# Block sums of batch 0 in other pairs, and a new order of issue, in a fused sparse attention and two-layer product on one core

## The chip, the core and the metric

The kernel runs on one core of a Trainium2 chip. The core has TensorE (PE) for matrix products, with weight loads shown apart as PEld; VectorE (DVE) and ScalarE (ACT) for elementwise work; GpSimd (POOL) and SyncE (SP), which here mostly issue transfers. The metric is the device time of one execution in microseconds (us); less is better. One execution in a set is also profiled, and from it come the page, the timeline and the waits quoted below. Its span runs from the first to the last recorded instruction.

## The reference

Four batches, 8 heads, 768 positions of 64 numbers. Each query attends to the keys less than 16 positions away and to 24 block keys (the elementwise maximum of 32 keys each, with weight log 32); a block's value is the mean of its 32 values. The result, 3072 rows of 512, goes through two products with a hard-swish between them.

```python
k_sum = k.reshape(B, H, nb, block, D).max(axis=3)       # block = 32, nb = 24
v_sum = v.reshape(B, H, nb, block, D).mean(axis=3)
scores_l = scale * q @ k^T, kept where |i - j| < 16
scores_s = scale * q @ k_sum^T + log(block)
a = softmax(concat(scores_l, scores_s))
x = a @ concat(v, v_sum)                                # 3072 x 512 after the heads are put side by side
h = x @ w_in                                            # 512 x 2048
out = (h * clip(h + 3, 0, 6) / 6) @ w_out               # 2048 x 512
```

## The kernel before

The work is built as a list of small steps, each with a name, an engine, and what it reads and writes. The string ORDER (lines 29 to 72) lists all steps by name; `Plan.run` walks it with written-out costs, gives each step its buffer and a planned begin, and sorts the steps by that begin. Each engine then runs its steps in the resulting order, in which it may wait but never overtakes. `:A` or `:D` behind a name puts a step that either engine can do on ACT or DVE. The names, with b a batch:

- K and Q, V, h, B with a batch number: loads of k, q, v, of the 32 rows of v ahead of each window (halo), and of v by blocks (batch 3 only), all issued by POOL. I and O are the weights of the two products (lines 499 and 505). Lines 447, 456, 467, 490, 493 and 725 are where loads of k and q, of v, of halos and of blocks are issued. Eight loads are in flight at most.
- k and q (b = 0): transposes on PE of raw keys and queries, with the copies out of PSUM and the maximum over blocks (line 559). For batches 1 and 2 DVE transposes instead (lines 617 and 623), and w makes the block maxima (778) and their copies; for batch 3 a crossbar transfer on SP's queue does it (599 and 608).
- s: scores on PE (649 for batch 0, 683 for the others), the exponential on ACT (660, 689), the band mask on DVE (691).
- u: block sums of v on PE (702 and 748) with their copies and spreads over the windows; U: the sums of batch 3 on DVE (735).
- v: attention times values (813 to 817 and 844), the normalisation on DVE (851, 852), and the transpose of x: on PE for batch 0 and the second half of batch 1, by a crossbar transfer on SP (line 857) for the rest. y (line 861) is a two-element copy on POOL that waits for the first crossbar transfer; the loads behind it start after that transfer has landed.
- F with stage and column group: the first product (928) into a PSUM buffer S, ACT's relu (934), DVE's product (936). A stage is half a batch, so stages 4 and 5 are batch 2. Two F steps of four matmuls each fill one S, called a pair below.
- G with stage and row group: the second product (950) in steps of four matmuls, the copy of the finished rows into one of four buffers ot (517, by ACT or DVE), and the store on SP (961, 962).

PSUM holds three S buffers of two banks and two single ones, h. PE has filler matmuls (line 1049) in the planned gaps of the first 27 us.

At the start, batch 0 is loaded and its attention computed while the weights arrive. From then on PE alternates between F and G of the finished stages and the scores, sums and values of the next batch. The loads of batches 1 to 3 run in one long queue behind. The crossbar transfer of x of stage 4 (v20.6 in ORDER) is the first of batch 2; F40 is its first reader. SP's queue holds the crossbar transfers and the stores in one order.

For batch 0 the block sums of four head pairs are made in two bursts of 24 matmuls (`vsum_first`, from line 983), each for two pairs:

```python
for cs in ((0, 2), (1, 3)):
    vsum_first(cs)
```

Of the kernel before, what the change touches and what calls it, by code (L numbers as in the profile page):

```python
# [9 lines left out]
F32 = mybir.dt.float32  # L10
# [5 lines left out]
D = 64  # L16
# [14 lines left out]
c.9 e.3 k01.1 k03.0 k02.0 q030.0 q020.0 k03.3:D c.4 q030.1:D k01.3:A k01.2:A q000.0 q010.0 k02.3:A k03.2:A k02.2:A V03.0  # L31
k03.1 k02.1 k02.4:D k01.4:D k00.0 q020.1:A q000.1:A k00.3:A s010.0 s030.0 q010.1:A s010.1 s010.2 s020.0 c.3 V01.0 V00.0 V02.0
I0.0 I2.0 I3.0 K10.0 I1.0 K13.0 K11.0 K12.0 O0.0 n.0:D k03.4:D s020.1 s030.1 s020.2 s030.2 k00.2:D k00.1 k00.4:D s000.0
q031.0 q001.0 q031.1:D q001.1:D h030.0:D h031.0:D h011.0:D h010.0:D s001.0 s000.1 s000.2 s001.1 q011.0 s001.2 s011.0 q021.0
q021.1:A q011.1:A s021.0 s031.0 s031.1 s021.1 s011.1 s031.2 s011.2 u01.0 h000.0:D u03.0:D u03.1:D u00.0 u01.1:A s021.2
u00.1:A u01.2:D h020.0:D u00.2:D u02.0:A u01.3:A u02.1:A h001.0:A u00.3:D h021.0:D O1.0 Q10.0 O2.0 Q11.0 Q13.0 Q12.0 v00.0
v01.0 v00.1 v02.0 v01.1 v02.1 v00.2 v00.3 v01.2 v02.2 v01.3 v00.4 v02.3 v03.3 v03.0 e.4 v03.1 v00.5:A v01.4 v02.4 v01.5:D
v02.5:A F00.0 F00.1 F00.2 F00.3 F00.4 F00.5 F00.6 v03.2 v03.4 v03.5 v03.6 F02.0 F02.1 F00.7 v03.7:A F02.2 F00.8 F00.9 v03.8
F00.10 F00.11 F00.12 F00.13 F02.4 F02.5 F00.14 c.5 F02.3 F00.15 F03.0 v03.9:A F02.6 F03.1 F03.2 F02.7 F03.3 F01.4 v03.10
v03.11:D F01.5 F01.6 F01.7 F03.4 F03.5 F03.6 F03.7 F10.0 F10.1 F10.2 F10.4 F10.5 F10.6 F10.3 F10.7 F01.0 F01.1 F11.4 F11.5  # L40
F01.2 k10.0 k13.0 F11.6 F01.3 F11.7 F11.0 k12.0 k11.0 G02.0 G10.0 F11.1 F11.2 F11.3 F13.0 F12.4 F12.5 F13.1 F13.2 F13.3 G02.1
w1.0 F12.6 F12.7 F12.0 F12.1 G10.1 F12.2 F12.3 G02.2 F13.4 F13.5 G01.0 F13.6 G10.2 O3.0 G11.0 G11.1 G11.2 G01.1 G01.2 G01.3
# [12 lines left out]
s230.2 u2.4:D u2.6:D s210.1 s200.1 s240.1 s240.2 u2.8:A s210.2 G22.0 F22.4 F22.5 s220.2 v20.0 v20.3 v20.1 v20.4 v20.2 v20.5
# [3 lines left out]
G21.5 k3e1.0 G30.5 k3e0.0 F40.5 F50.0 G20.3 F50.1 F50.4 F50.5 U3.4:A F40.6 F50.2 G20.4:A u3.4:D F40.7 F50.6 F52.4 F52.5  # L59
G22.4:D w3.3:D F50.3 F50.7 F52.6 F52.7 F42.4 F42.5 F53.4 F53.5 G40.0 F51.0 F51.1 u3.7:A F42.6 F53.6 w3.4:A u3.6:A w3.0 F53.7  # L60
F42.7 q3x1.0 G22.5 G32.5 q3x0.0 F51.2 F51.3 u3.1:A F51.4 F51.5 F51.6 u3.5:A F52.0 F52.1 F52.2 G41.0 G41.1 G40.1 G41.2 w3.1
F51.7 F52.3 w3.2:A s300.0 s300.1 s320.0 s350.0 s350.1 s320.1 G40.2 G41.3 G40.3 s350.2 G41.4:D G40.4:D s300.2 s310.0 u3.2:A
s310.1 s310.2 s320.2 u3.3:D s330.0 s340.0 s330.1 s340.1 G52.0 G52.1 G52.2 v33.3 v33.0 v33.1 v33.2 v33.4 F53.0 F53.1 u3.0:A
# [170 lines left out]
def kernel(  # L234
# [461 lines left out]
    def vsum_first(cs):  # L696
        T = Buf(("h", "S"))

        def mms():
            for t in range(NQ):  # L700
                for i, c in enumerate(cs):
                    nc.tensor.matmul(bank(T)[BLK * i:BLK * i + BLK, 0:2 * D], ind[:, t], vaug[0][0:WIN, 2 * c:2 * c + 2, t, 0:D],
                                     start=(t == 0), stop=(t == NQ - 1))
        plan.at(f"u0{cs[0]}")
        op("PE", mm(NQ, 2 * D), mms, form="sums", r=["ind"] + [(n, 0, c) for n in ("v", "vz") for c in cs], w=[T], alloc=T,
           touch=[rows0[c, x] for c in cs for x in range(2)])
        for i, c in enumerate(cs):
            spread_first(c, i, T)
# [385 lines left out]
```

## Time and profile before

| | us |
|---|---|
| three runs | 218.68, 216.0, 215.9 |
| median | 216.0 |
| the profiled execution, whole | 217.25 |
| its span | 215.6 |
| granted clock of PE | 0.999 of full speed |
| matmuls on PE | 2082 |

In the page a group of instructions is given by line, engine, operation and what it reads and writes; behind the count stand the busy time, the mean duration in ns, and the idle time before them with the engine that ended it. "issue" means that the profile shows nothing that the engine waited for. The timeline gives the start, the duration, the engine and line, and merges neighbours of one kind.

The stages can be read from the busy time in stretches (busy us and instructions of PE, PEld, DVE, ACT, POOL; then the granted clock, the share of the transfer engines, and GB/s):

```profile
0.00:10.00 10.00, 8.46 (x82) 3.76 (x82) 5.88 (x22) 5.49 (x12) 8.62 (x19) 1.00 0.90 123
20.00:30.00 10.00, 9.48 (x208) 7.37 (x203) 9.18 (x22) 6.81 (x12) 3.48 (x5) 1.00 1.71 186
50.00:60.00 10.00, 10.00 (x49) 4.57 (x47) 9.93 (x13) 3.54 (x6) 4.75 (x5) 1.00 2.35 151
100.00:110.00 10.00, 8.45 (x173) 4.78 (x172) 5.86 (x12) 8.64 (x10) 2.59 (x4) 1.00 1.76 139
120.00:130.00 10.00, 7.87 (x47) 4.60 (x48) 6.30 (x7) 4.54 (x6) 0.00 (x0) 1.00 0.79 164
150.00:160.00 10.00, 10.00 (x138) 5.28 (x136) 7.18 (x12) 7.43 (x9) 0.00 (x0) 1.00 0.15 55
```

PE is busy throughout most stretches; it has gaps at the start, between 100 and 110, and between 120 and 130.

### The profile page before, as it was taken

What the parts mean: (1) busy time and instruction counts of PE and PEld (TensorE: products, weight loads), DVE (VectorE), ACT (ScalarE), POOL (GpSimd) and SP (SyncE); (2) the same over time, 40 slices, a digit from 0 to 9 for tenths busy, and PEclk for the clock granted to TensorE, in tenths of its full rate; (3) what the DMA queues carried; (4) which work ended last, traced back from release to release, by engine and by line L of the source; (5) the groups of instructions that cost most, each with busy time, mean ns of one, the idle gap of its engine ahead of it and who ended that gap; (6) DMA issues with size and microseconds to landing.
All of it is one profiled execution on the core that took longest, in us unless ns stands there. A gap on an engine that the chain in (4) does not pass through costs nothing.

```text
span 215.6 us, 4886 instructions
## 1 busy us (share of the span) xinstructions
PE 204.8 (95%) x2082; PEld 115.7 (54%) x2082; DVE 154.0 (71%) x236; ACT 115.7 (54%) x163; POOL 69.2 (32%) x84
## 2 busy tenths in 40 slices
PE   7989999999999999999799599999999999999993
PEld 2555776555446665555455265655555555665442
DVE  6697887879988899997568579985785453633321
ACT  5679665533399567367980154798921541551101
POOL 7999335455446209779142000000000000000000
PEclk9999999999999999999999999999999999999999
DMA  4999999999999979999939999720223600100234
GB/s 68 184 156 195 182 159 159 181 138 157 147 122 149 112 131 135 177 163 162 171 28 148 123 197 152 124 49 2 100 42 83 170 0 3 49 0 15 97 126 155
DMA packets 120598, 25.40 MB, mean 118 GB/s; under 512 B 111424, under 2 KB 117440, under 8 KB 120576
## 3 DMA queue, kind: packets, MB, share of 16 engines
q0 software_dynamic: 102656, 15.26, 106.9%
q1 hardware_dynamic: 17920, 9.83, 19.4%
q8 instruction: 16, 0.26, 0.5%
q14 instruction: 6, 0.05, 0.1%
HBM read 30.51 MB, written 6.29 MB: 171 GB/s over the span
## 4 chain that ended last, share of the span: by engine, by line
PE 87%; DMA 4%; DVE 4%; issue 2%; ACT 1%; SPq 1%; DVEq 0%; ACTq 0%
PE S L928 38%; PE h L950 27%; PE S L950 8%; DMA out_dram<-ot 4%; PE h L1049 3%; PE S L844 3%; PE S L683 2%; DVE vaug L521 1%; PE h L538 1%; PE S L638 1%; PE S L649 1%; DVE qwide L852 1%; SPq L857 1%; ACT at L660 0%; PE h L910 0%
## 5 line engine op out<-in xcount | busy, mean ns | idle before, releaser
L928 PE MATMUL S<-x,win 128*128 128x384 bf16 (+1 forms) x544 | 88.2, 317 | 3.0 <-ACT ot L517 1.4
L934 ACT ACTIVATE r<-S 128x768 f32<-128x768 f32 x64 | 51.3, 810 | 56.6 <-PE S L928 53.8
L936 DVE SCALAR_TENSOR_TENSOR g<-r,S 128x768 bf16<-128x768 f32 x64 | 59.6, 947 | 21.0 <-ACT r L934 20.8
L928 PEld LDWEIGHTS <-win 128*128 128x128 bf16 x544 | 50.9, 98 | 37.1 <-issue 2.1
L950 PE MATMUL h<-wout,g 128*128 128x512 bf16 (+2 forms) x304 | 68.3, 365 | 0.0
L950 PEld LDWEIGHTS <-g 128*128 128x128 bf16 x416 | 38.5, 98 | 39.5
L950 PE MATMUL S<-wout,g 128*128 128x512 bf16 (+1 forms) x112 | 23.9, 356 | 0.0
L689 ACT ACTIVATE at<-S 120x1024 bf16<-120x1024 f32 x18 | 17.3, 1024 | 1.8 <-PE S L683 1.7
L467 POOL DMA_DIRECT2D vaug<-in_v_dram x16 | 15.4, 965 | 5.6 <-issue 4.1
L691 DVE TENSOR_TENSOR at<-at,mask 96x1024 bf16<-96x1024 bf16 x18 | 11.8, 680 | 4.4 <-ACT at L689 4.3
L456 POOL DMA_DIRECT2D nat<-in_q_dram x8 | 10.5, 1317 | 13.7 <-issue 9.0
L517 ACT COPY ot<-h 128x512 f32<-128x512 f32 (+2 forms) x12 | 6.5, 542 | 15.0 <-PE h L950 15.0
L456 POOL DMA_DIRECT2D nat<-in_k_dram x8 | 10.6, 1339 | 4.1 <-issue 4.1
L517 ACT COPY vaug<-vs 24x768 bf16<-24x768 bf16 x14 | 11.6, 828 | 0.3
L778 DVE TENSOR_REDUCE red<-kb 128x48 bf16<-128x1536 bf16 x6 | 10.5, 1745 | 0.0
L517 DVE COPY ot<-h 128x512 f32<-128x512 f32 x7 | 4.7, 686 | 7.6 <-PE h L950 4.7
L1049 PE MATMUL h<-g 128*128 128x512 bf16 x25 | 8.6, 486 | 1.5 <-DVE g L327 1.5
L517 ACT COPY ot<-S 128x512 f32<-128x512 f32 x3 | 1.8, 585 | 13.3 <-DMA out_dram<-ot 9.8
L517 DVE COPY ot<-S 128x512 f32<-128x512 f32 (+1 forms) x4 | 2.4, 592 | 7.8 <-PE S L950 7.8
L521 DVE TENSOR_TENSOR vaug<-vaug 32x768 bf16<-32x768 bf16 (+2 forms) x22 | 7.8, 413 | 0.1
L735 DVE TENSOR_REDUCE total<-nat 128x32 f32<-128x1024 bf16 x4 | 7.6, 1900 | 0.0
L852 DVE TENSOR_TENSOR xm<-S,rc 128x768 bf16<-128x768 f32 x8 | 7.5, 945 | 0.1
(111 smaller groups left out, 172.5 us busy)
## 6 DMA issues: line engine op xcount, KB each, us to landing
out_dram<-ot SPq DMA_DIRECT2D x19, 256.0 KB, 2.3
vaug<-in_v_dram POOLq DMA_DIRECT2D x16, 192.0 KB, 7.4
win<-in_moe_w_in_dram POOLq DMA_DIRECT2D x4, 512.0 KB, 10.8
wout<-in_moe_w_out_dram POOLq DMA_DIRECT2D x4, 512.0 KB, 17.0
nat<-in_k_dram POOLq DMA_DIRECT2D x10, 192.0 KB, 9.0
nat<-in_q_dram POOLq DMA_DIRECT2D x10, 192.0 KB, 13.2
out_dram<-ot SPq DMA_DIRECT2D x4, 224.0 KB, 2.6
nat<-in_k_dram POOLq DMA_DIRECT2D x6, 128.0 KB, 6.9
```

The lines of the kernel that those rows point to most:

```text
L456: op("POOL", 1.35, over=0.01, fn=lambda src=src, name=name, hs=hs, ds=ds, rows=rows: nc.gpsimd.dma_start(out=raw[b % 2][name][rows], in_=s ...
L467: op("POOL", 0.945, lambda: nc.gpsimd.dma_start(out=o[BLK:WIN, lo:hi, 0:D], in_=rows[:, lo:hi]), w=[("v", b % 2, c)], dma=1.28, els=1536)
L517: {"ACT": nc.scalar.copy, "DVE": nc.vector.tensor_copy, "POOL": nc.gpsimd.tensor_copy}[eng](o, i)
L521: nc.vector.tensor_tensor(o, i, i, op=ALU.max)
L689: op("ACT", 1.02, lambda: nc.scalar.activation(odds[0:KEYS, :, w], X.slot[0:KEYS], AF.Exp, scale=scl), r=[X], w=[("atg", k)])
L691: op("DVE", 0.69, lambda: nc.vector.tensor_tensor(odds[0:WIN, :, w].rearrange("p j (t c) -> p j t c", c=QB), odds[0:WIN, :, w].rearrange(" ...
L778: nc.vector.tensor_reduce(red.slot[:].rearrange("x (p u e n) -> x e u p n", p=NP, u=NS, e=2)[:, e], w[:, n * e:n * e + n, BLK:WIN].rearran ...
L928: nc.tensor.matmul(h.slot[:, f, lo * 128:hi * 128].rearrange("p (u c) -> p u c", c=128), w_in_sb[:, kt, (ft + f) * 128:(ft + f + 1) * 128] ...
L934: op("ACT", 0.81, lambda: nc.scalar.activation(r.slot[:], h.slot[:, :, 0:HALF], AF.Relu, bias=0.5, scale=1.0 / 6.0), r=[h], w=[r], alloc=r)
L936: op("DVE", 0.955, lambda: nc.vector.scalar_tensor_tensor(gt[s].slot[:, ft:ft + 2], r.slot[:], 1.0, h.slot[:, :, 0:HALF], op0=ALU.min, op1 ...
L950: nc.tensor.matmul(bank(o)[:, a:z], gt[s].slot[:, ft, ts * 128:(ts + 1) * 128], w_out_sb[:, ft, a:z], start=(ft == 0), stop=(ft == NFT - 1))
L1049: nc.tensor.matmul(o, idle[:, 0:128], idle[:], start=True, stop=True)
```

## The change

Two things change. The block sums of batch 0 are made for pairs (0, 1) and (2, 3) instead of (0, 2) and (1, 3). And the string ORDER is another one: the same steps, in another order and in part on the other of the two engines. No step is added or taken away, apart from fillers: the first 27 us hold 19 instead of 26, so PE has 2075 matmuls. The first lines of the string, and the lines around the crossbar transfer of x of batch 2, cut:

```diff
-K01.0 K02.0 Q010.0 c.1 c.2 Q000.0 K00.0 Q01w0.0 Q01w1.0 Q01w2.0 k01.0 c.0 z1.0:D e.2 c.8 f.0 c.7 z2.0:D e.1 e.0 z0.0:A z3.0:A
+K01.0 K02.0 Q010.0 c.2 Q000.0 c.1 K00.0 Q01w2.0 Q01w1.0 Q01w0.0 k01.0 c.0 z1.0:D c.9 z3.0:D e.2 e.4 e.0 c.7 e.1 z2.0:A z0.0:A
...
-I0.0 I2.0 I3.0 K10.0 I1.0 K13.0 K11.0 K12.0 O0.0 n.0:D k03.4:D s020.1 s030.1 s020.2 s030.2 k00.2:D k00.1 k00.4:D s000.0
+h010.0:D f.0 h031.0:D h030.0:D I0.0 K11.0 I1.0 I2.0 O1.0 I3.0 K13.0 K10.0 K12.0 O0.0 Q11.0 Q12.0 Q13.0 O2.0 Q10.0 O3.0 s031.0
...
-s230.0 s230.1 s220.1 s250.1 y10.0 h21.0 K34.0 h20.0 h30.0 V21.0 Q30.0 K33.0 Q33.0 V23.0 h22.0 B31.0 V32.0 V31.0 B30.0 K31.0
-Q34.0 V33.0 K32.0 K30.0 B32.0 B33.0 h31.0 G30.0 G30.1 u2.0 s200.0 s210.0 s240.0 u2.1:D u2.2:D u2.7:D s250.2 G30.2 G30.3
...
-s200.2 G30.4:A u2.9:A F22.6 u2.3:A u2.5:A F22.7 G20.0 G20.1 G21.0 G21.1 v20.6 G31.5 v23.3 v23.0 G20.2 G21.2 G21.3 G22.1
-G21.4:A v23.1 U3.3 v23.4 v23.2 U3.2 v23.5 F40.0 F40.1 F41.4 F41.5 F40.2 F41.6 F40.3 F41.7 F42.0 F42.1 F42.2 F42.3 F41.0 F41.1
-F43.4 F43.5 F41.2 F43.6 U3.0 F41.3 F43.7 U3.1 F40.4 G22.2 G22.3 F43.0 F43.1 F43.2 F43.3 h32.0 V30.0 K35.0 Q31.0 Q35.0 v23.6
...
+G30.0 G31.2 G31.3 G30.1 w2.2:A s240.0 s240.1 G31.4:D s250.0 s230.0 y10.0 h20.0 Q32.0 V30.0 Q33.0 V20.0 V22.0 h22.0 K31.0
+h30.0 B33.0 V21.0 G30.2 F22.0 F22.1 s250.1 s230.1 F22.2 F22.3 G30.3 u2.0 s210.0 s220.0 s200.0 G30.4:A s210.1 s240.2 s220.1
...
+F22.7 u2.3:D u2.6:D F23.6 F23.7 s200.1 v20.0 v20.3 s200.2 v20.4 v20.1 u2.5:D v20.2 v20.5 B31.0 K32.0 Q35.0 h31.0 K35.0 K33.0
+Q31.0 V32.0 K34.0 B32.0 B30.0 h32.0 V31.0 Q34.0 Q30.0 V33.0 G21.0 G21.1 G22.2 G22.3 v23.3 v23.0 G20.2 G20.3 G21.2 G21.3 v20.6
+G30.5 G21.4:A U3.2 v23.1 v23.4 U3.3 v23.2 U3.0 v23.5 F40.0 F40.1 F40.2 F41.4 F41.5 F41.6 F40.3 F41.7 G00.5 v23.6 q3x0.0 F41.0
...
-    for cs in ((0, 2), (1, 3)):
+    for cs in ((0, 1), (2, 3)):
         vsum_first(cs)
```

In the engines' own queues this gives, around batch 2: behind y both programs have 28 load instructions on POOL. Before, the 24th to 28th are h32, V30, K35, Q31 and Q35, and h32 stands right behind h31; now h31 is the 15th and h32 the 23rd. On PE, 12 matmuls of G that stood behind F40 stand ahead of it. On SP, both crossbar transfers of x of batch 2 keep their stores between them, and two transfers of batch 3 (one of q, one of k) now follow directly on the second.

More of the change, by code (lines that the diff above doesn't have):

```diff
@@ L59 @@
[L59 to L63, printed above, removed]
@@ new lines @@
+u02.0 s000.2 u01.0:A u00.1:A u00.2:A u01.2:D u01.1:D u02.1:A u03.0:A h020.0:D s001.2 u00.3:A u03.1:A v00.0 v00.1 v02.0 v01.0
+v01.1 v02.1 h021.0:D v00.2 u02.2:D v00.3 v00.4 v01.2 v02.2 v01.3 v02.3 v03.3 v03.0 v03.1 v00.5:A v01.4 v02.4 v01.5:D v02.5:A
+F00.0 F00.1 F00.2 F00.3 F00.4 F00.5 F00.6 v03.2 v03.4 v03.5 v03.6 F00.8 F00.9 F00.10 F00.11 F00.12 F00.13 v03.7:D v03.8 F01.0
+v03.10 F01.1 F00.14 F00.7 F00.15 F02.0 F02.1 v03.11:A v03.9:D F01.2 F02.2 F01.3 F02.3 F10.0 F10.1 F10.2 F10.3 F10.4 F10.5
@@ new lines @@
+F10.6 F10.7 F11.0 F11.1 F11.2 F11.3 F12.4 F12.5 F12.6 F12.7 F03.4 F03.5 F03.6 F03.7 c.5 F01.4 F01.5 F02.4 F02.5 F01.6 F02.6
+F01.7 k12.0 F02.7 F12.0 F12.1 F11.4 F11.5 F11.6 F11.7 F12.2 F13.4 G11.0 F13.5 F13.6 k10.0 F12.3 F13.7 F03.0 F03.1 k11.0 F03.2
+F03.3 G02.0 G01.0 k13.0 w1.0 w1.1 F13.0 F13.1 F13.2 F13.3 q12.0 w1.4:A w1.3:A w1.2:A G01.1 G10.0 G10.1 G01.2 G10.2 G11.1
+G02.1 G02.2 G10.3 V12.0 V10.0 V13.0 V11.0 q11.0 q13.0 q10.0 q14.0:D G01.3 G01.4:D G02.3 G11.2 G11.3 h100.0:D h121.0:D G02.4:D
@@ new lines @@
+G10.4:A h120.0:A h101.0:A h131.0:A c.6:D h111.0:D h110.0:D h130.0:D G11.4:A h21.0 K20.0 Q23.0 K22.0 Q21.0 K21.0 K23.0 K30.0
+Q20.0 V23.0 Q22.0 s120.0 s130.0 s110.0 G00.0 G00.1 s130.1 s120.1 s110.1 u1.0 s100.0 s150.0 s140.0 u1.1:A s100.1 s140.1 u1.9:A
+G12.0 G00.2 G12.1 s130.2 s120.2 u1.5:D u1.3:D s110.2 s100.2 u1.7:D v13.0 v13.3 u1.8:D v13.1 v13.2 v13.4 v13.5 s140.2 u1.2:A
+s150.1 s150.2 u1.6:A u1.4:A G00.3 v13.6 G12.2 G12.3 v13.7:A v13.10 v13.8 v13.11:D v10.3 v10.0 v10.1 v10.4 v10.2 v10.5 G11.5
@@ new lines @@
+G30.5 G21.4:A U3.2 v23.1 v23.4 U3.3 v23.2 U3.0 v23.5 F40.0 F40.1 F40.2 F41.4 F41.5 F41.6 F40.3 F41.7 G00.5 v23.6 q3x0.0 F41.0
+F41.1 F41.2 F41.3 F42.0 F42.1 F42.2 G20.4:A F42.3 F40.4 F40.5 F40.6 F40.7 k3e0.0 G21.5 G32.5 k3e1.0 q3x1.0 G31.5 G20.5 F42.4
+F42.5 F42.6 F42.7 F50.0 F50.1 F52.4 F52.5 F50.2 F52.6 F50.3 F52.7 G22.4:D F51.4 F51.5 F50.4 F50.5 F51.6 F51.7 F50.6 F50.7
+F43.0 F43.1 F43.2 F53.0 F43.3 w3.0 G41.0 F51.0 F53.1 F53.2 F53.3 F51.1 F53.4 F53.5 F51.2 F53.6 G41.1 w3.1 F43.4 F53.7 F51.3
@@ new lines @@
+F43.5 F43.6 F43.7 U3.1 w3.4:D w3.3:D G41.2 F52.0 G40.0 F52.1 G40.1 G41.3 G40.2 G40.3 F52.2 w3.2:D G41.4:D F52.3 G40.4:A
+s350.0 s300.0 s320.0 s300.1 s320.1 U3.4:A s350.1 u3.7:A u3.6:A G50.0 G50.1 G52.0 G52.1 s310.0 s340.0 s330.0 G52.2 G52.3 G50.2
+s310.1 s340.1 u3.4:A u3.2:A s330.1 u3.0:D s300.2 s350.2 s320.2 u3.1:D s310.2 u3.3:D u3.5:D v33.0 v33.3 G52.4:D G51.0 G51.1
+v33.4 v33.1 v33.2 s340.2 v33.5 G42.0 G42.1 G51.2 G51.3 G42.2 s330.2 v30.0 v30.1 v30.2 v30.3 v30.4 v30.5 G42.3 G52.5 G41.5
+G22.5 v33.6 F70.0 F70.1 F70.2 G51.4:A F71.0 F71.1 F71.2 G42.4:D v30.6 G51.5 F70.3 F71.3 F71.4 F71.5 F71.6 F71.7 F70.4 F70.5
@@ new lines @@
+F72.4 F72.5 F70.6 F70.7 F60.0 F60.1 F63.4 F63.5 G50.3 F60.2 F60.3 F63.6 F72.6 F63.7 F61.0 F61.1 F72.7 G72.0 F61.2 F73.4 F73.5
+F73.6 G50.4:A F61.3 F73.7 F72.0 F72.1 F72.2 F72.3 F73.0 F73.1 F63.0 G71.0 F61.4 F63.1 F61.5 F73.2 F73.3 F63.2 F63.3 G71.3
+F61.6 F61.7 F62.4 F62.5 F62.0 G71.1 G71.6 F62.6 F62.7 G71.9 G72.1 G71.4 G72.2 G71.7 F60.4 F62.1 G71.12 G71.13:A F60.5 G72.3
+G70.0 G70.1 G70.2 F60.6 F60.7 F62.2 F62.3 G60.0 G60.1 G70.3 G61.0 G71.14 G42.5 G70.4:D G60.2 G72.4:D G70.5 G72.5 G60.3
+G60.4:D G60.5 G71.10:D G71.11 G40.5 G50.5 G62.0 G62.1 G62.2 G61.1 G61.2 G61.3 G62.3 G61.4:D G61.5 G62.4:D G62.5 G71.2 G71.5
@@ L72 @@
+G71.8 G71.15 G71.16:A G71.17
 """
```

39 lines of the change are left out of this document (9 added, 30 removed).

## The prediction

> **What bounds the kernel now.** I began with the page's table of busy time and the list of what TensorE (PE) waited for.
>
> ```profile
> PE 204.8 (95%) x2082; PEld 115.7 (54%) x2082; DVE 154.0 (71%) x236; ACT 115.7 (54%) x163; POOL 69.2 (32%) x84
> ...
> PE S L683 <- issue: 1.6, 1, 1.6
> PE S L928 <- ACT ot L517: 1.4, 1, 1.4
> PE S L928 <- DMA x<-qwide: 1.2, 1, 1.2
> PE S L928 <- DVE x L517: 0.3, 1, 0.3
> ```
>
> PE sets the time: 204.8 of 215.6 us busy. The matmuls that carry results are the same before and after, so the change can win only in PE's idle time (10.8 us), in the filler matmuls of the start, and in the tail behind the last matmul. Three waits of the steady part are large enough to matter: 1.6, 1.4 and 1.2 us. The timeline places them; its columns are start, duration, engine, line, operation, and in brackets the idle time before and what ended it.
>
> ```profile
> 100.57 0.88 PE L683 MATMUL S<-q,kb 64*128 64x64 bf16 x48
> 103.21 0.85 PE L748 MATMUL h<-vaug,ind 96*32 96x128 bf16 x48
> 106.37 0.23 PE L683 MATMUL S<-q,kb 64*128 64x64 bf16 x4 [1.55 <-issue]
> 110.52 0.95 PE L844 MATMUL S<-vaug,at 120*64 120x65 bf16 x48
> 113.49 1.37 SPq L857 DMA_TRANSPOSE x<-qwide  x1
> 114.91 1.18 SPq L962 DMA_DIRECT2D out_dram<-ot  x1
> 120.70 1.47 PE L928 MATMUL S<-x,win 128*128 128x384 bf16 x8 [1.23 <-DMA x<-qwide]
> 122.97 0.58 ACT L517 COPY ot<-S 128x512 f32<-128x512 f32 x1 [9.76 <-DMA out_dram<-ot]
> 123.61 6.01 PE L928 MATMUL S<-x,win 128*128 128x384 bf16 x36 [1.43 <-ACT ot L517]
> ```
>
> The first wait lies inside a burst of scores of batch 2: 44 of 48 matmuls ran, then nothing for 1.55 us, and no releaser is named. The other two belong together. SP issues the crossbar transfer of x of batch 2 at 113.49 (I call it the turn). F40 (first product, first half of batch 2) waits for it until 120.70. A store issued behind the turn lands at 122.9, which keeps an output buffer, then ACT's copy of G21, then a PSUM bank, and PE waits another 1.43. Why the turn was slow is in the rows of the transfers (number, KB, us from issue to landing), the first and last for the stretch 103 to 118:
>
> ```profile
> nat<-in_q_dram POOLq DMA_DIRECT2D x2, 128.0 KB, 6.3
> x<-qwide SPq DMA_TRANSPOSE x1, 7.2
> x<-xm SPq DMA_TRANSPOSE x3, 3.7
> ...
> 81.12 0.94 POOL L490 DMA_DIRECT2D vaug<-in_v_dram  x1 [0.32 <-issue]
> 102.01 0.96 POOL L490 DMA_DIRECT2D vaug<-in_v_dram  x1
> 110.59 0.60 POOL L493 DMA_DIRECT2D vaug<-in_v_dram  x1 [7.62 <-DMA vaug<-in_v_dram]
> 113.00 1.77 POOL L447 DMA_DIRECT2D nat<-in_q_dram  x2
> vaug<-in_v_dram POOLq DMA_DIRECT2D x1, 188.0 KB, 8.3
> ```
>
> A turn takes 3.7 us, this one took 7.2, and landed (113.49 + 7.2 = 120.7) 0.5 after the last q load (113.9 + 6.3 = 120.2). POOL had stood 7.62 us before h32 (L493), which waits for h31, issued just ahead at 102.01 and landed 8.3 later; so five loads of batch 3 came at 110.6 to 114.8, beside the turn.
>
> **The change, part by part.** *Loads and turn.* In both programs 28 load instructions follow POOL's small copy (L861). Before, the first 23 took from 81.12 to 110.3 (102.01 + 8.3): 29.2 us, 1.27 each. In the new order h32 comes eight loads behind the load that it waited for, so POOL doesn't stand there, and an unbroken queue ends near 81.1 + 28 x 1.27 = 116.7. The turn moves too. Twelve matmuls of the second product (G) that stood behind F40 now stand ahead of it.
>
> ```profile
> 52.35 0.86 PE S L950 x4
> 34.38 7.80 PE S L928 x48
> ```
>
> From these rows of the chain of waits, four G matmuls are 0.86 us and twelve 2.6; eight F matmuls (one pair) are 1.30. So the values of batch 2 (L844, 110.52 before) start at 110.52 - 1.55 + 2.6 = 111.6 if the first wait goes. Between them and F40 the order has the same matmuls in both programs: 48 values, 16 G, 48 values, 16 G. That took 120.70 - 1.23 - 110.52 = 8.95 us, so PE reaches F40 at 120.5. The turn was issued 2.97 after the values began (113.49 - 110.52); a copy of 24x768 on DVE now stands between, 0.35 (row below), so it is issued at 114.9 and lands at 118.6 by the 3.7 of an undisturbed turn, or 0.5 behind the last load, 117.2. Both are before 120.5: 1.23 gained, with 1.9 us of cover. If the cover goes, each us costs one.
>
> *The output buffer.* G21's copy still waits for the store of G30, which stays behind the turn on SP. Before, that store landed 2.2 us after the turn (122.9 - 120.7); now at 118.6 + 2.2 = 120.8, and G21's copy (0.58) ends at 121.4. PE misses that bank only after two pairs of F4, 120.5 + 2.6 = 123.1: 1.43 gained, 1.7 of cover. DVE gets a third block sum (L735) ahead of the second half's scaling, 1.9 us:
>
> ```profile
> L735 DVE TENSOR_REDUCE total<-nat 128x32 f32<-128x1024 bf16 x4 | 7.6, 1900 | 0.0
> L517 DVE COPY vaug<-vs 24x768 bf16<-24x768 bf16 x6 | 2.1, 353 | 0.2
> L778 DVE TENSOR_REDUCE red<-kb 128x48 bf16<-128x1536 bf16 x6 | 10.5, 1745 | 0.0
> L517 ACT COPY kb<-red 128x1152 bf16<-128x1152 bf16 x3 | 3.5, 1151 | 0.9 <-DVE red L778 0.9
> L936 DVE SCALAR_TENSOR_TENSOR g<-r,S 128x768 bf16<-128x768 f32 x64 | 59.6, 947 | 21.0 <-ACT r L934 20.8
> ```
>
> The second turn moves from 121.70 to about 123.2 and lands by 127. F50, its reader, comes six pairs after F40 begins, at 120.5 + 7.8 = 128.3: free.
>
> *The wait inside the scores.* The row has no releaser. The trace's list of queues, though, has a 16 KB block on the queue "instruction" under way at 103.5 to 103.75 and none from 82 until then:
>
> ```profile
> q8 instruction: 1, 0.02, 24.4%
> ```
>
> I take the wait for code that came late. Counted in PE's instruction order the stop is at instruction 2494. The 256 (16 KB at 64 bytes, an inference) before it began near 100.9 and were through at 104.8, while the next were there at 106.4, 5.5 us after 100.9. In the new order these 256 hold a pair of F and four G more between the two bursts: 0.2 + 0.86 + 1.30 + 0.86 + 0.78 + 0.81 + 0.8 = 5.6 us. So the 5.5 are just covered, and I take the whole 1.55; the bounds are 0 and 1.55. [...]
>
> *The start.* Here no single row decides; I followed ACT, which is in order from the first exponential to the first values of batch 0.
>
> ```profile
> 1.53 4.02 PE L1049 MATMUL h<-g 128*128 128x512 bf16 x9 [1.53 <-DVE g L327]
> 5.48 0.85 PE L538 MATMUL h<-ident,nat 96*64 96x96 bf16 x16
> 3.82 0.29 POOL L322 TENSOR_SCALAR_AFFINE_SELECT ident<-ident 128x128 bf16<-128x128 bf16 x1
> 13.38 2.23 ACT L660 ACTIVATE at<-S 120x768 bf16<-120x768 f32 x3 [0.44 <-PE S L649]
> 21.89 0.41 PE L813 MATMUL S<-vaug,at 120*64 120x65 bf16 x15 [0.17 <-DVE vaug L521]
> 25.84 0.61 PE L928 MATMUL S<-x,win 128*128 128x128 bf16 x8
> ```
>
> The identity is now built behind the mask band and a q load, ready near 5.8 instead of 4.1, and a tenth filler (4.02/9 = 0.45) stands ahead: the first transposes slip from 5.48 to 5.85. But q of pair 1 is copied earlier on ACT, so the first exponential starts near 12.6 instead of 13.38. From there ACT does seven exponentials (2.23/3 = 0.74 each), three q copies, one maximum, two sums and one spread, 8.3 us by its rows, to 20.9; DVE ends its two spreads at 21.2, and the values start at 21.3 instead of 21.89. DVE then has two halos and one spread between the normalisations, which before came earlier, and gives the gain back: the first product starts 0.15 sooner by my count. As it hangs on twenty short steps, I keep -0.6 and +0.5 as ends. The new pairing of sums itself costs nothing: 48 matmuls in two bursts, as before, and v of all pairs is in by then.
>
> *Elsewhere* a burst of scores of batch 1 loses one interruption (0.1). DVE's queue ahead of batch 2's scores is full: by the 947 and 1745 ns above its last maximum ends at the moment of the scores, with ACT's 1.15 us copy behind it. Back to back, DVE's operations overlap by some 0.08 (two g in 1.79), which over 25 of them frees 2 us. I take 0, ends 0 and 1.2. The tail is alike: last copy 128 columns on ACT, then one store.
>
> ```profile
> 77.01 1.78 DVE L936 SCALAR_TENSOR_TENSOR g<-r,S 128x768 bf16<-128x768 f32 x2
> 212.01 0.27 ACT L517 COPY ot<-h 128x128 f32<-128x128 f32 x1 [0.31 <-PE h L950]
> ```
>
> Sum: 1.23 + 1.43 + 1.55 + 0.15 + 0.1 = 4.5 us. The profiled execution took 217.25, 215.6 of it span; the median of the runs, 216.0, lies 0.4 above the span. So 211.1 of span, and 211.5 as median.
>
> **The rivals.** (1) The turn is freed, but the wait in the scores stays, or a like one comes elsewhere (DVE's queue ahead of batch 2's scores): 211.5 + 1.5 = 213.0, between 212.4 and 214. For it: no releaser is shown, and 5.6 against 5.5 is no margin. (2) The change doesn't do what it says: the loads still land beside the turn. At more than 120 us (1.39 per load instead of 1.27, or a start later by 3 us) turn and store come as late as before, and 211.5 + 1.23 + 1.43 + about 1 for the start's upper end and small waits = 215.2. Against it: the queue never ran dry from 82 to 109, and the 3 us are more than anything ahead of it moves. (3) Slower: POOL's order. V21, the last v load of batch 2, now stands behind B33, which must wait until DVE has turned all k and q of batch 2 (before, B31 stood so at 92.84, with batch 2's v loads already issued). V21 then lands some 8 us after that release (8.3 in the row of its kind above); the sums of batch 2 (L748) need it at about 103.5. It decides from 95.5 on; each us later costs one, and pushes the rest of the 18 loads, so the turn and F40, too. With DVE done at 92.8 as before it costs nothing; 4 us later it costs 1.3, the last loads end near 121, and with the waits of (2) the time is 216.5; at 9 us later 221.5.
>
> ```profile
> 92.84 0.62 POOL L725 DMA_DIRECT2D nat<-in_v_dram  x1 [1.60 <-DVE q L623]
> ```
>
> **How the numbers follow.** Forecast 0.55 (210.4 to 212.6, from the start's ends and part of the code wait); rival 1 0.20 (212.4 to 214); rival 2 0.12 (214 to 216.5); rival 3 0.13 (216.5 and over). 2% of 216.0 is 4.3 us, about what a measurement of this kernel can tell from no change: so the bounds are 211.7 and 220.3. Three quarters of the forecast's case lie under 211.7, 0.41; over 220.3 lies most of rival 3, 0.10, as a delay of POOL's queue grows down its length; the rest, 0.49, is within: the forecast's upper end, rivals 1 and 2, and the lower part of rival 3. I predict 211.5. The range 210.4 to 216.0 leaves out rival 3, a little of rival 2, and a start beyond its lower end: some 0.2.
>
> **What would show it.** Right: the turn of x of batch 2 lands in under 5 us, no PE wait for it or for ACT's ot copy, no gap in L683, the first L928 at 25.2 to 26.3. Wrong: a turn of 6 us or more with POOL's loads still landing, a gap of a us or more in the scores or ahead of the sums of batch 2, L725 waiting beyond 95, or a first L928 after 26.4.

## The result, and the profile after

Nine runs of the changed kernel have a median of 214.94 us (213.67 to 217.99), nine of the kernel before beside them 216.82 (215.9 to 218.68): 1.9 us less, where 4.5 were forecast. The ratio, 0.9886 with a 95% interval of 0.9844 to 0.9928, leaves out the run of 217.99, which is over 1.5% above the fastest; by it the changed kernel is faster by 1.1%, inside the 2% that the prediction took for no change. The profiled execution took 215.34, 213.6 of it span: 2.0 less than before. In the table of busy time and the list of what PE waited for (total, times, longest, in us) the lines that answer to those shown of before are:

```profile
PE 204.7 (96%) x2075; PEld 116.4 (54%) x2075; DVE 158.4 (74%) x241; ACT 110.9 (52%) x158; POOL 69.2 (32%) x84
...
PE S L844 <- issue: 1.4, 1, 1.4
PE S L817 <- issue: 0.4, 1, 0.4
PE S L928 <- ACT ot L517: 0.3, 1, 0.3
PE S L928 <- DMA x<-qwide: 0.2, 1, 0.2
```

The two waits behind the crossbar transfer have nearly gone (1.43 to 0.27, 1.23 to 0.22). The unnamed wait in the scores (L683, 1.55) has gone too, but two unnamed waits stand in other places: 1.39 in the values of batch 1 (L844) and 0.41 in those of batch 0 (L817). The timeline of the changed kernel places all this:

```profile
20.64 0.32 PE L813 MATMUL S<-vaug,at 120*64 120x65 bf16 x8 [0.24 <-ACT vaug L517]
...
23.26 0.31 PE L817 MATMUL S<-g,at 24*64 24x65 bf16 x8 [0.41 <-issue]
...
24.05 1.53 PE L844 MATMUL S<-vaug,at 120*64 120x65 bf16 x48
...
26.33 1.76 PE L928 MATMUL S<-x,win 128*128 128x128 bf16 x24
...
68.98 0.89 PE L844 MATMUL S<-vaug,at 120*64 120x65 bf16 x44
71.26 0.25 PE L844 MATMUL S<-vaug,at 120*64 120x65 bf16 x4 [1.39 <-issue]
...
106.12 0.88 PE L683 MATMUL S<-q,kb 64*128 64x64 bf16 x48
...
109.74 0.94 POOL L467 DMA_DIRECT2D vaug<-in_v_dram  x1 [0.58 <-DMA nat<-in_k_dram]
...
113.09 0.95 PE L844 MATMUL S<-vaug,at 120*64 120x65 bf16 x48
...
116.89 1.29 SPq L857 DMA_TRANSPOSE x<-qwide  x1
...
122.26 1.47 PE L928 MATMUL S<-x,win 128*128 128x384 bf16 x8 [0.22 <-DMA x<-qwide]
...
123.37 0.59 ACT L517 COPY ot<-S 128x512 f32<-128x512 f32 x1 [10.12 <-DVE total L735]
...
124.01 1.30 PE L928 MATMUL S<-x,win 128*128 128x384 bf16 x7 [0.27 <-ACT ot L517]
```

POOL's last load is issued at 109.74, seven us ahead of the turn (116.89). PE comes to F40 at 122.26 - 0.22 = 122.04, which is 8.95 behind the values (113.09): the forecast stretch, to the hundredth. The start is late: the first L928 stands at 26.33 instead of 25.84, although the first values begin at 20.64 instead of 21.89. Between the two PE stopped for 0.41, and then ran slowly: 48 values took 1.53 instead of 1.17. The lines of the kernel before that answer to these are:

```profile
24.28 1.17 PE L844 MATMUL S<-vaug,at 120*64 120x65 bf16 x48
...
26.77 1.05 PE L928 MATMUL S<-x,win 128*128 128x128 bf16 x16 [0.32 <-DVE x L517]
```

The busy time in stretches of one us (the seventh entry behind the stretch, ahead of the last two, is the granted clock) shows why:

```profile
23.00:24.00 1.00, 0.74 (x12) 0.54 (x12) 0.76 (x4) 0.45 (x1) 0.33 (x1) 0.73 1.24 202
24.00:25.00 1.00, 1.00 (x36) 0.96 (x36) 0.98 (x2) 0.59 (x1) 0.76 (x1) 0.50 1.25 207
25.00:26.00 1.00, 1.00 (x27) 0.94 (x22) 0.23 (x1) 0.00 (x0) 0.00 (x0) 0.50 1.23 206
26.00:27.00 1.00, 1.00 (x14) 1.00 (x12) 0.85 (x2) 0.42 (x1) 0.82 (x1) 0.56 1.30 224
```

PE's clock was halved for 3.4 us, from 23.5 to 26.9. So the span's 2.0 us are: 1.01 and 1.16 from the turn, 1.55 - 1.39 = 0.16 from the unnamed waits in the steady part, and the start's loss, taken off: 0.28, as read from the steady F stages behind it (less than the 0.49 at the first L928, since the kernel before waits 0.32 for x there, which the changed one does not). 1.01 + 1.16 + 0.16 - 0.28 = 2.05.

### The profile page after: what moved, and what is told of

Read it like the earlier page. It is cut to its first block, busy times and chain, and to the rows that moved or that the text cites. A ratio compares the mean times of both kernels' runs of the same rounds, so it can differ in the third digit from the quotient of the medians.

```text
span 213.6 us, 4873 instructions
## 1 busy us (share of the span) xinstructions
PE 204.7 (96%) x2075; PEld 116.4 (54%) x2075; DVE 158.4 (74%) x241; ACT 110.9 (52%) x158; POOL 69.2 (32%) x84
## 4 chain that ended last, share of the span: by engine, by line
PE 83%; DVE 8%; ACT 5%; issue 2%; ACTq 0%
PE S L928 37%; PE h L950 23%; PE S L950 12%; PE h L1049 3%; DVE total L735 2%; PE S L844 2%; PE S L683 2%; ACT at L660 2%; ACT at L689 1%; DVE g L936 1%; DVE qwide L852 1%; ACT vaug L517 1%; PE h L748 1%; PE h L910 1%; ACT q L517 1%
## 5 line engine op out<-in xcount | busy, mean ns | idle before, releaser
L928 PE MATMUL S<-x,win 128*128 128x384 bf16 (+1 forms) x544 | 88.2, 317 | 0.5 <-ACT ot L517 0.3
L928 PEld LDWEIGHTS <-win 128*128 128x128 bf16 x544 | 51.3, 98 | 34.2 <-issue 0.8
L950 PE MATMUL h<-wout,g 128*128 128x512 bf16 (+2 forms) x272 | 60.7, 364 | 0.0
L950 PE MATMUL S<-wout,g 128*128 128x512 bf16 (+1 forms) x144 | 30.7, 361 | 0.0
L517 ACT COPY ot<-h 128x512 f32<-128x512 f32 (+1 forms) x10 | 5.5, 552 | 18.0 <-PE h L950 18.0
L517 DVE COPY ot<-S 128x512 f32<-128x512 f32 x6 | 4.1, 690 | 9.0 <-PE S L950 6.7
L517 ACT COPY ot<-S 128x512 f32<-128x512 f32 (+1 forms) x3 | 1.4, 479 | 17.4 <-DVE total L735 10.1
L844 PE MATMUL S<-vaug,at 120*64 120x65 bf16 x336 | 7.5, 203 | 1.4 <-issue 1.4
L844 PEld LDWEIGHTS <-at 120*64 120x64 bf16 x336 | 6.5, 118 | 3.9 <-issue 2.5
L517 ACT COPY vaug<-vs 24x768 bf16<-24x768 bf16 x10 | 8.2, 828 | 0.2
L617 DVE STREAM_TRANSPOSE kb<-nat 128x768 bf16<-128x768 bf16 x8 | 7.7, 965 | 0.0
```

Of the source, the lines that this page charges most:

```text
L517: {"ACT": nc.scalar.copy, "DVE": nc.vector.tensor_copy, "POOL": nc.gpsimd.tensor_copy}[eng](o, i)
L844: nc.tensor.matmul(X.slot[64 * c:64 * c + 64, e, (D + 1) * y:(D + 1) * (y + 1)], odds[0:KEYS, j, u * QB:(u + 1) * QB], vaug[b % 2][0:KEYS, ...
L928: nc.tensor.matmul(h.slot[:, f, lo * 128:hi * 128].rearrange("p (u c) -> p u c", c=128), w_in_sb[:, kt, (ft + f) * 128:(ft + f + 1) * 128] ...
L950: nc.tensor.matmul(bank(o)[:, a:z], gt[s].slot[:, ft, ts * 128:(ts + 1) * 128], w_out_sb[:, ft, a:z], start=(ft == 0), stop=(ft == NFT - 1))
```

## The experiments

The question was why the unnamed wait moved rather than went. The code theory of the prediction says that PE stops where a block of 256 instructions begins that has not arrived; the rival is a hidden releaser of the step in which the wait is seen. The second question was the turn, the third the start. The table has the medians of four to ten runs; "before" is the kernel before on the same chip (216.84, 216.78 and 216.71 in the three groups); the last column has the waits without a releaser and those of the turn, from the profiled execution:

| run | median us | ratio, 95% interval | unnamed waits; waits for x, for ot |
|---|---|---|---|
| shift192 | 212.8 | 0.982, 0.9746 to 0.9894 | L817 0.40; -, 0.31 |
| shift128 | 213.28 | 0.983, 0.9765 to 0.9894 | none |
| before_shift192 | 214.76 | 0.9892, 0.985 to 0.9934 | L928 0.22; 0.26, 1.02 |
| before_h32 | 214.7 | 0.9897, 0.9818 to 0.9976 | L683 2.20; none |
| fill5 | 214.01 | 0.9865, 0.9833 to 0.9897 | L683 0.86; -, 0.30 |
| fill5_shift128 | 212.61 | 0.9811, 0.979 to 0.9833 | none |
| before_h32_shift192 | 212.72 | 0.9829, 0.9799 to 0.9859 | none |
| pairs_only | 216.52 | 1.0001, 0.9961 to 1.0041 | L683 1.84; -, 0.96 |
| before_shift32 | 215.07, one run | | none; 1.81, - |
| h32_back | 214.76 | 0.992, 0.9893 to 0.9948 | L844 1.01; 0.89, 0.28 |
| fill2_shift128 | 213.51 | 0.9851, 0.9823 to 0.9879 | L815 0.38, L928 0.24; none |

**More instructions in the changed kernel.** Some F0 matmuls are cut in three, which adds instructions and nearly no work (shift192: ft under 16, shift128: ft under 12):

```diff
         def mms(f, lo, hi):
-            for kt in range(NP):
-                nc.tensor.matmul(h.slot[:, f, lo * 128:hi * 128].rearrange("p (u c) -> p u c", c=128), w_in_sb[:, kt, (ft + f) * 128:(ft + f + 1) * 128],
-                                 xt[s].slot[:, lo:hi, kt], start=(kt == 0), stop=(kt == NP - 1))
+            for a, z, kt in [(a, z, kt) for a, z in (zip(range(lo, hi), range(lo + 1, hi + 1)) if s == 0 and 4 <= ft < 16 else [(lo, hi)]) for kt in range(NP)]:
+                nc.tensor.matmul(h.slot[:, f, a * 128:z * 128].rearrange("p (u c) -> p u c", c=128), w_in_sb[:, kt, (ft + f) * 128:(ft + f + 1) * 128],
+                                 xt[s].slot[:, a:z, kt], start=(kt == 0), stop=(kt == NP - 1))
```

> The changed kernel, with the 48 matmuls of 384 columns of the third to eighth pair of F0 (first product, first tile, from about 28 us) each cut into three of 128 columns: the same sums and the same order on every engine, but 192 more instructions in PE's stream from there on, and about 0.4 us more matmul time (3 x 57 ns against 162 ns, 48 times). Code theory (PE stops at every 256th instruction when the 256 before it were used up faster than the next block arrives, 5.5 to 6.2 us): the stretches between 31 and 200 us now take 6.9 us of work at least, so the wait of 1.39 in the values of batch 1 (L844) goes and none comes for it; time 214.9 - 1.4 + 0.4 = 213.9. Rival (the wait belongs to the values of batch 1, by a releaser that the trace doesn't name): it stays at 1.4; time 215.3.

The wait of 1.39 went and none came for it. At 212.8 the kernel gained 2.1 instead of the expected 1.0 against 214.94. The wait for x went too, the one for ot stayed (0.31). But not all of the 2.1 is the cut: in the profiled execution PE's clock was halved for 3.4 us, as in the profile after, and its span of 212.9 is only 0.7 shorter. The other three runs had a whole clock, against three of nine of the changed kernel, which is worth about a us (see the start, below).

> The same edit for the third to sixth pair of F0: 128 more instructions, about 0.3 us more matmul time. Code theory: the boundary that lay four matmuls before the end of the values of batch 1 now lies eight matmuls before the end of the second last scores burst (L683, near 66 us) of batch 1, and the 256 instructions before it take only 3.7 us; so PE stops there, 40 of 48 matmuls into that burst, for 5.9 - 3.7 = 2.2 us (between 1.5 and 2.6), and the values run through; time 214.9 - 1.4 + 0.3 + 2.2 = 216.0. Rival: the wait stays in the values, 1.4, and the scores run through; time 215.2.

Half of this held. The values run through, but the expected stop in the scores did not come, as the timeline shows:

```profile
65.35 0.87 PE L683 MATMUL S<-q,kb 64*128 64x64 bf16 x48
66.16 2.76 PE L950 MATMUL h<-wout,g 128*128 128x512 bf16 x12
68.85 0.95 PE L844 MATMUL S<-vaug,at 120*64 120x65 bf16 x48
```

The boundary lies eight matmuls before the end of that burst, 3.9 us behind the one before it, and PE didn't stop. So the rule "under 5.5 us it stops" is wrong, while the hidden releaser of the values is refuted: the step is the same, and its wait is gone.

**The same in the kernel before.**

> The kernel before, with the same edit for the third to eighth pair of F0 (192 more instructions, 0.4 us more matmul time). Code theory: the 256 instructions ahead of the wait of 1.55 in the scores of batch 2 (3.7 us of work) are split over two stretches of 6.3 us or more, the wait goes, none comes; time 216.8 - 1.55 + 0.4 = 215.7. Rival (it belongs to those scores): it stays at 1.5; time 217.2.

The scores run through, and the median fell by 2.1, more than the 1.15 expected. PE came to the values earlier, so the turn was issued at 112.38 and took 6.2 us; its waits fell to 0.26 and 1.02 from 1.23 and 1.43. None of its ten runs has a mean clock under 0.996, while six of the 13 beside it have 0.992 or less, so a part of the 2.1 may be the clock. A stop of 0.22 came in F0 (L928, 29.65).

> The kernel before with the third pair of F0 alone cut into three parts: 32 more instructions. Code theory: the boundary that fell four matmuls before the end of the scores burst at 106 us now falls 16 matmuls earlier (two instructions to a matmul); the 256 ahead of it still hold 3.7 us of work, and the block ahead of that place was behind its boundary by 5.4 to 6.1 us in three runs; so this burst is broken in two, 28 matmuls and 20, with a gap of 1.4 to 2.3 us between them. Rival (any cause that belongs to the step, or to its 44th matmul): the gap is again ahead of the last 4, or there is none. Time as before within 0.5.

Missed: there is no gap at all in that burst, though its boundary lies 3.9 us behind the last. In this run the turn of x (7.8 us) is late by 1.81 instead.

**Where the stops are, and when.** All eleven unnamed stops of 0.2 us and more behind 20 us, in thirteen traces, can be placed by counting matmuls (two instructions each) in PE's order. They stand ahead of instruction 703 (three), 959 (two), 1727 (two) and 2493 (four): within one matmul, 703 and multiples of 256 behind it. They lie in five different lines. Where four instructions were added ahead (two fillers, fill2_shift128), the stop at 703 moved two matmuls ahead, out of L817 into L815, and the next came 256 later in the middle of F0:

```profile
22.32 0.28 PE L815 MATMUL S<-vaug,at 96*64 96x65 bf16 x6
22.98 0.22 PE L815 MATMUL S<-vaug,at 96*64 96x65 bf16 x2 [0.38 <-issue]
...
28.40 0.28 PE L928 MATMUL S<-x,win 128*128 128x128 bf16 x2
28.91 0.73 PE L928 MATMUL S<-x,win 128*128 128x128 bf16 x10 [0.24 <-issue]
```

The place is thus settled. That PE stops there for code is my reading of it, and it rests on two measurements: the blocks in the table below, and the list of queues of the kernel before, which has 16 blocks on the queue "instruction", 0.26 MB in all or 16 KB each, for PE's 4164 instructions (2082 matmuls and as many weight loads), 260 to a block and 63 bytes to an instruction, near the 64 that the prediction inferred:

```profile
q8 instruction: 16, 0.26, 0.5%
```

When it stops is not a matter of the work between two boundaries alone (4.77 us with a stop, 4.74 without, in the first and the third row below). For these passages I set beside each other when PE passed the boundary before, when the queue "instruction" had a 16 KB block under way (read in stretches of 0.1 to 0.25 us), when PE came to the next boundary and when it went on:

| kernel | passes | block | at the next | goes on |
|---|---|---|---|---|
| after | 65.10 | 68.6 | 69.87 | 71.26 |
| h32_back | 63.65 | 66.65 | 68.41 | 69.42 |
| kernel before | 64.86 | 65.96 | 69.6 | at once |
| shift128 | 62.20 | 62.5 | 66.06 | at once |
| after | 102.04 | 105.04 | 107.71 | at once |
| kernel before | 100.94 | 103.64 | 104.82 | 106.37 |
| before_h32 | 101.41 | 104.31 | 105.29 | 107.49 |
| pairs_only | 101.54 | 104.44 | 105.42 | 107.26 |
| fill5 | 99.73 | 103.13 | 104.76 | 105.62 |
| before_shift32 | 101.19 | 99.75 | 105.06 | at once |

In these rows, where PE stopped, it went on 2.5 to 3.2 us behind the block; where 2.67 us or more were left from block to boundary, it didn't stop. But the block itself comes between 1.4 us ahead of the passage and 3.5 behind it. What sets that (the other transfers of the moment are an obvious candidate) wasn't tried and stays open. The traces show a tendency: from 20 us on each has one such block for every 256 instructions of PE, 186 in all thirteen that can be set beside a passage. Where the transfer engines moved under 10 GB/s within two us of the passage (21 of them), the block started between 3.0 us ahead of it and 0.6 behind, 2.0 ahead at the median; where they moved 175 GB/s or more (44), between 1.7 ahead and 4.1 behind, 3.0 behind at the median.

**The turn, one edit each way.** In the kernel before, the second halo load was put behind the four loads that follow it (in ORDER, V30.0 K35.0 Q31.0 Q35.0 h32.0 now stand ahead of v20.0); in the changed kernel, the two halo loads were put together again ahead of the last four loads:

```diff
-    order = plan.run()
+    order = plan.run(); back = [o for o in order if o.key in ('h31.0', 'h32.0')]; order = [x for o in order if o not in back for x in (back if o.key == 'V31.0' else []) + [o]]
```

> The kernel before, with one edit on POOL's queue alone: the four last loads of batch 3 (v of pair 0, k of one group, q of two) are issued ahead of the second halo load h32, which waits for h31, instead of behind it. Theory (loads beside the turn made it slow, and it made both waits): the loads are issued from 103 instead of 110.6 and have landed before the turn of x of batch 2 is issued at 113.5; it takes under 5 us instead of 7.2; PE's waits of 1.23 (x, ahead of F40) and 1.43 (ot, ahead of the next pairs) go; time 216.8 - 2.7 = 214.1. Rival (the turn is slow for another reason, or the time is given back in a later wait): turn still over 6 us, or new PE waits of 1.5 us and more; time 215.5 to 217.

In the timeline F40 and the pairs behind it run without a wait; the row below it is the transfer's own (number, and us from issue to landing):

```profile
107.49 0.23 PE L683 MATMUL S<-q,kb 64*128 64x64 bf16 x4 [2.20 <-issue]
...
114.61 1.29 SPq L857 DMA_TRANSPOSE x<-qwide  x1
...
119.57 1.03 PE L950 MATMUL h<-wout,g 128*128 128x512 bf16 x4
120.43 4.88 PE L928 MATMUL S<-x,win 128*128 128x384 bf16 x29
```

```profile
x<-qwide SPq DMA_TRANSPOSE x1, 3.7
```

3.7 us instead of 7.2, and 214.7 instead of 216.84, with the unnamed stop at 2.20 in place of 1.55 in this profile. So the two waits came from POOL's stand: no other queue's order differs.

> The changed kernel with POOL's two halo loads h31 and h32, one right behind the other, ahead of the last four loads, as in the kernel before; every other queue stays. Theory of the order: h31 is issued at 103.7, lands near 111.5, POOL stands for it, the four loads are issued at 112 to 116 and land up to 122, beside the turn of x of batch 2 issued at 116.9; the turn takes 5 to 7.2 us, F40, which PE reaches at 122.0, waits up to 2, and the next pairs for ot 0.3 to 1.7: 216.6 (215.2 to 218). Rival (cover of two us hides it, and the gain came from the other moves of the new order): turn under 5 us or PE waits under 0.5 in sum; 214.9.

Missed: 214.76 is the changed kernel's own time, though not at a like clock: its three runs at a whole clock (214.21, 214.39, 214.76) are 0.4 longer on the mean than those of the changed kernel (213.67, 214.0, 214.58), too few to tell. POOL stood, but for 6.32 us, and a part of the waits returned:

```profile
109.41 0.60 POOL L493 DMA_DIRECT2D vaug<-in_v_dram  x1 [6.32 <-DMA vaug<-in_v_dram]
...
115.49 1.28 SPq L857 DMA_TRANSPOSE x<-qwide  x1
...
121.29 1.48 PE L928 MATMUL S<-x,win 128*128 128x384 bf16 x8 [0.89 <-DMA x<-qwide]
123.04 2.27 PE L928 MATMUL S<-x,win 128*128 128x384 bf16 x13 [0.28 <-ACT ot L517]
```

The transfer took 5.8 us (121.29 - 115.49) and F40 waited 0.89 instead of 0.22. The last loads were issued at 113.4, two us ahead of the turn, and F40 has 12 G matmuls ahead of it. I take it that these moves of the new order hide most of what the stand would cost; no run separates them. Moving h32 alone removes both waits (before_h32); the other moves without it bring them from 2.66 to 1.17.

**The start.** Fillers are put between the second burst of sums and the first values (results unused), five or two of them:

```diff
-            n = int(max(min(o.begin, SLOW) - end, 0.0) / 0.43 + max(o.begin - 0.15 - max(end, SLOW), 0.0) / 0.22) + (end == BEGIN["PE"])
+            n = {'k01.0': 10, 'k03.0': 4, 'q011.0': 2, 'q030.0': 1, 'u02.0': 2, 'v00.0': 5}.get(o.key, 0)
```

> The changed kernel with five filler matmuls (512 columns, results unused) put back between the second burst of block sums and the first values of batch 0, where the kernel before has five and the changed one none. Clock theory (the granted clock halved at 23.3 to 26.6 because PE had too little to do from 20.3 on): clock 1.00 in every stretch from 20 to 28; the fillers take 1.25 us, of which 0.2 lie in a wait, so the values start at 21.6 instead of 20.6, but then run as in the kernel before (3.95 us from the first values to the first L928): first L928 at 25.6 instead of 26.3. The boundary ahead of L817 moves by ten instructions and the block has a us longer: no stop there. The stop in the values of batch 1 (now nine matmuls before their end) stays at 1.2 to 1.6. Time 214.9 - 0.8 = 214.1. Rival (the clock falls whatever PE does there, or the start is bound by ACT and DVE): clock 0.5 in two stretches or more, first L928 at 26.5 or later, 215.2 to 216.

The clock stayed whole, the first L928 is at 25.64 (25.6 expected) and the median 214.01:

```profile
23.00:24.00 1.00, 0.63 (x19) 0.47 (x20) 0.97 (x5) 0.47 (x1) 0.49 (x1) 1.00 1.24 207
24.00:25.00 1.00, 1.00 (x48) 0.87 (x48) 1.00 (x2) 0.58 (x1) 0.27 (x1) 1.00 1.24 205
25.00:26.00 1.00, 1.00 (x32) 0.96 (x25) 0.84 (x4) 0.15 (x1) 0.17 (x1) 1.00 1.23 205
```

The stop in the values of batch 1 did not stay, though; one of 0.86 came at the boundary 2493 instead.

> Both edits on the changed kernel: the five fillers, and the 32 matmuls of F0 each cut into three (128 instructions more). If they add: no PE wait of over 0.5 us behind 12 us, first L928 at 25.6, clock 1.00 from 20 to 28; 213.3 (measured with the cut alone) - 0.8 = 212.5. Rival (fillers only move the start's loss): 213.3 or more. By the code theory no block is more than 2.7 us behind a boundary by more than PE has work for, so no stop of over 0.3 us.

212.61, 2.3 us under the 214.94 of the changed kernel: faster than both kernels. The two edits nearly add up: against 214.94 they win 0.93 and 1.66 alone and 2.33 together. The first L928 is later than expected, at 26.10, as PE waited 0.63 at 8.03 for a load of k in this execution.

> As the run with five fillers and 128 more instructions (212.6), with two fillers in place of five: 0.5 us of matmuls, half of it in a wait. If two are enough for the clock: values start at 20.9, first L928 at 25.1, 212.1. Rival (two are too few): clock 0.5 in at least one stretch of 23 to 27, first L928 at 25.9 or later, 213.0.

Two fillers kept the clock (0.998 to 1.0 in the five runs), and the first L928 came at 25.27, but the stop at 703 returned with 0.38, the runs spread from 212.46 to 214.09, and the median is 213.51. Five is the better number.

The mean granted clock over a whole execution tells in which runs PE was slowed. Of the nine runs of the changed kernel six have 0.982 to 0.992; of the thirteen with fillers none is under 0.997. With the three other kernels that have the changed start (shift192, shift128 and h32_back), ten of the 22 runs without fillers have 0.992 or less. Such runs are longer on the mean: by 0.9 us in the changed kernel (217.99 left out), by 1.4 in pairs_only. But the fillers are not all of it: of the 35 runs of the kernel before beside the experiments, which has five there, nine have 0.992 or less, and of the ten of pairs_only, with the same five, five. The profiled run of h32_back, without fillers, kept a whole clock and had no stop at 703; it shows what the start could be:

```profile
22.98 0.31 PE L817 MATMUL S<-g,at 24*64 24x65 bf16 x8
...
23.65 1.08 PE L844 MATMUL S<-vaug,at 120*64 120x65 bf16 x48
24.66 0.62 PE L910 MATMUL h<-ident,xn 128*128 128x128 bf16 x8
25.12 1.51 PE L928 MATMUL S<-x,win 128*128 128x128 bf16 x24
```

The first L928 at 25.12 is 1.21 ahead of the 26.33 of the changed kernel's profile: 0.28 of it at L817 (22.98 instead of 23.26, without the stop), the other 0.93 in the matmuls behind it, at the whole clock.

**The pairs alone, and both single edits on the kernel before.** In the first, the block sums of batch 0 take the new pairs in the old places:

```diff
-    for cs in ((0, 2), (1, 3)):
+    for cs in ((0, 1), (2, 3)):
         vsum_first(cs)
```

> The kernel before with the other half of the change alone: the block sums of batch 0 by pairs (0,1) and (2,3), their operations in the places of the old ones, the same fillers in the same places, every queue else as before. If the pairing costs nothing: 216.8 within 0.3, first values and first L928 within 0.15 us of 21.89 and 25.84, the waits of 1.55, 1.23 and 1.43 there as before. Rival (it is the pairing that starts the values earlier and opens the gap in which the clock falls): first values at 21.5 or earlier, first L928 off by 0.3 or more.

No cost shows in the time: 1.0001 of the time before, within 0.4%. Of the three waits the profile has 1.84 in the scores, none for x and 0.96 for ot. The places are off by more than expected: the first values at 22.24, the first L928 at 26.85. Some 0.6 of that is there ahead of the second burst already (its fillers start at 19.74 instead of 19.15), where PE had waited 0.42 at 8.21 for a load of k, ahead of any block sum; and then the transposes wait 0.55 for DVE:

```profile
19.74 0.60 PE L1049 MATMUL h<-g 128*128 128x512 bf16 x2
...
22.24 0.44 PE L813 MATMUL S<-vaug,at 120*64 120x65 bf16 x16
...
25.05 0.40 PE L910 MATMUL h<-ident,xn 128*128 128x128 bf16 x4 [0.55 <-DVE xn L897]
...
26.85 1.35 PE L928 MATMUL S<-x,win 128*128 128x128 bf16 x20
```

Most of the first 0.6 is thus this execution's. Whether the wait for DVE is the pairing's stays open; the earlier first values of the changed kernel (20.64) do not come from the pairing.

> The kernel before with both single edits that were measured alone: POOL's halo load h32 behind the four loads, and 192 more instructions from the third pair of F0. If the three waits are separate sums: 1.23 + 1.43 (turn) and 1.55 (code) all go, 0.4 is added; 216.8 - 4.2 + 0.4 = 213.0, with no PE wait of over 0.5 us between 30 and 205 us. Rival (one gives back what the other wins): 214 or more, with a new wait.

212.72: the three waits of the kernel before are separate sums. That kernel has neither the new pairs nor the new order, only one load moved and 48 matmuls cut.

## Why the prediction was wrong

The direction was right, and so was the mechanism of the largest part; the size was not, 1.9 where 4.5 were forecast.

- **The turn of x (1.23).** Right in cause and nearly in size: 1.01 came. Its cover of 1.9 us was used up, since the transfer took 5.4 us (122.26 - 116.89) instead of 3.7 and was issued 3.8 behind the values instead of 3.3, and 0.22 of wait was left. These 5.4 us are not the loads' doing: the trace has no packet of POOL's loads from 115.3 on, 1.6 ahead of the turn. What else made the transfer slow is not shown.
- **The output buffer (1.43).** Right: 1.16 came, by the chain that was forecast.
- **The unnamed wait (1.55).** This is the step that failed: "So the 5.5 are just covered, and I take the whole 1.55". At that one boundary it held, but by luck: shift128 shows that 5.5 us between boundaries are not the rule, and what counted was that the block was under way at 105.04, 2.67 before PE needed it. The step that went wrong is to book the whole 1.55 from one boundary: in the thirteen traces stops came at four places, multiples of 256 instructions apart within one matmul, and I examined one. The boundary at 1727 had 4.8 us behind it in both kernels; the block was early enough before and late after. With the 0.41 at 703 the changed kernel lost 1.80 to such stops, the kernel before 1.55: instead of a gain of 1.55, a loss of 0.25 (the sum below counts the 0.41 with the start). Rival 1 said this ("or a like one comes elsewhere"), with 0.20.
- **The start (0.15).** Wrong in sign: 0.28 lost. ACT's and DVE's steps were well counted, the first values came even 0.7 earlier than forecast, and in h32_back the first product was 0.57 ahead of the forecast 25.69 (25.84 - 0.15). What failed is that PE was taken as only waiting there: the seven fillers that the change drops were given no price, and with a stop of 0.41 and a clock halved for 3.4 us the start gave the gain back in the profiled run; six of the nine runs have the lowered clock.
- **The rest (0.1).** Nothing of it shows; the pairing and DVE's queue cost nothing that the time shows, as taken. Rival 3 did not occur: POOL's load B33 waited to 93.68, ahead of the 95.5 from which it decides, and the v load behind it went at 94.38.

The sum is 2.05 instead of 4.46. The 2.41 that lack are 1.39 in the code wait that came at another boundary, 0.43 in the start, 0.49 in what the turn and the output buffer left, and 0.1 in the rest.

## What to carry to other kernels

Where a wait has no releaser and lies inside a burst of like instructions, count its place in the engine's instruction order. If its places lie a fixed number of instructions apart, as here (703, 959, 1727 and 2493, multiples of 256 apart within one matmul), it belongs to the count and not to the step: edits ahead moved it here by two matmuls (four instructions more, fill2_shift128) or took 1.39 us of it away (128 more, shift128). So a gain or a loss of a us from such a wait is luck, and both kernels must be searched at every such place before either is credited. Some added or cut instructions ahead of a dense stretch can be worth as much as a new schedule (214.76 in before_shift192, 214.94 in the changed kernel), and filler matmuls that a schedule drops can have a price in the clock: without them six of the nine runs of the changed kernel have a mean clock of 0.982 to 0.992, with them none of thirteen is under 0.997.

## What the runs showed of the hardware that was not expected

Where PE stopped in the rows above, it went on 2.5 to 3.2 us after the block was seen under way, and the block came up to 3.5 us behind PE's passage into the block before. Four more instructions ahead of a stop moved it by two matmuls. In the changed kernel PE's clock fell to half at 23.5 us; PE had been busy for 0.72, 0.85 and 0.85 of the three us from 20 to 23, and its longest idle time there and up to 23.5 was 0.41:

```profile
20.00:21.00 1.00, 0.72 (x24) 0.54 (x19) 0.97 (x3) 0.98 (x3) 1.00 (x1) 1.00 2.86 149
21.00:22.00 1.00, 0.85 (x29) 0.71 (x30) 0.85 (x5) 0.95 (x3) 0.21 (x1) 1.00 2.50 155
22.00:23.00 1.00, 0.85 (x32) 0.65 (x31) 0.97 (x2) 1.00 (x2) 0.99 (x1) 1.00 1.48 198
```

In shift128 it fell at 23.2 and in shift192 at 25.0, for 3.4 us each time, and in h32_back, with the same matmuls at the start, not at all; what decides is not shown.

The same crossbar transfer of x took 5.8 to 7.8 us in the five traces in which 0.2 MB and more of POOL's loads landed in the five us behind its issue (h32_back, pairs_only, before_shift192, the kernel before, before_shift32), and 4.6 in before_h32_shift192 with 0.1. In the seven in which all loads had landed ahead of it, it took 3.7 (before_h32) to 5.3 and 5.4 (the changed kernel and fill5). It took 4.1 in shift128, which has the same queues as the changed kernel; that difference stays open.
